# Second-layer weights of the first block group made among the last plain experts, in a pool of their own; two plain pairs exchanged; conversions of x begun at earlier steps

## The chip, the cores and the metric

One core of one Trainium2 chip runs the whole program. The metric is device microseconds from start to end of an execution; less is better. The engines are TensorE (PE, matrix products; PEld is its weight load), VectorE (DVE), ScalarE (ACT), GpSimd (POOL) and the queue of SyncE (SP), which issues the DMAs. Each engine works through its own instructions in a fixed order and waits, where it must, for semaphores of the others.

## The reference

```python
def _attn_ref(q, k, v, f_logit):             # (4, 8, 768, 48) each
    f = 1.0 / (1.0 + np.exp(-f_logit))
    for t in range(S):
        state = f[:, :, t, :, None] * state + np.einsum('bhd,bhe->bhde', k[:, :, t], v[:, :, t])
        y[:, :, t] = np.einsum('bhd,bhde->bhe', q[:, :, t], state)

def _moe_ref(x, w_gate, w1, w2):             # x is y as (3072, 384); 8 experts, 384 -> 1024 -> 384
    logits = x @ w_gate
    P = np.exp(logits - logits.max())
    for _ in range(8):
        P /= P.sum(1, keepdims=True) + 1e-09
        P /= P.sum(0, keepdims=True) + 1e-09
        P *= N / E
    for e in range(E):
        h = np.maximum(x @ w1[e], 0.0)
        ye = h @ w2[e]
        out += P[:, e:e + 1] * ye
```

A gated linear attention makes x. The gate's logits are balanced by eight rounds over rows and columns (P), and every expert is applied to every token, weighted with P.

## The kernel before

Everything is computed with pairs of fp16 numbers, a high part and a low part (names that end in h and l), and three products for one. The work has three stages, which overlap.

**Attention and tiles.** 24 steps of the recurrence make x as high and low parts (`xh`, `xl`, one pair of tiles for each of four batches b). While they run, products of the experts 0 and 1 with finished tokens fill TensorE.

**Plain experts.** Tokens come in eight units u, two for each batch. A *pair* (e, u) of `RAW` is expert e on unit u: eight first-layer groups (`hps`, 9 matmuls each, whose result ACT turns into `hh`, L423, and DVE into `hl`, L424) and three second-layer groups (`yps`, 24 matmuls each, which read all eight `hh` and `hl`). The order of matmuls is pinned: `mm` puts each behind the one before, and `pin` does the same on the other engines, so the order in which the Python code issues instructions is the order on each engine. Beside the last six pairs the main loop runs other generators, one piece of each per *step*. A step is 8 matmuls of the pairs (`LEAD`):

- `balance`, the eight rounds on P (L148 to L161; `sk_` names). In each round DVE makes column sums `sk_cs` (L153), TensorE adds them over partitions in one small product `sk_c`, which is issued in the pinned order 5 matmuls into the next step, and DVE goes on with its result (L157). At the end DVE makes `pes`.
- `convert(b)`, which turns x of a batch into the blocks that the third stage multiplies: `x32` = `xh` + `xl` (L1034, three instructions, on POOL for b = 0, 1 and on DVE for b = 2, 3), 17 sums on POOL (L1048, `xs`) with three maxima on DVE among them (L1051, `xmx`), and then high parts on ACT (L1067) and low parts on DVE (L1070: `xal` three times, `xbl` twice). `convert(0)` begins at step 0, the others at the steps in `CONVSTEP`. The low parts of a batch wait until its pairs are through, since they overwrite `xh` and `xl`.
- `prepare_w1` for the first two quarters of expert 2's first layer, at step `KSTEP`: a load (`k1r`), 10 sums on POOL (`k1s`), a maximum on DVE (L1105, `wmx`), ACT's high parts (L1112, `k1h`) and four low parts on DVE (L1115, `k1l`).

When the pairs up to the third from the end are issued, the pool with expert 0's weights is closed and the pool `kw` for `k1` opens in its space.

**Block groups.** For experts 2 to 7 the products are made by a scheme with 15 instead of 18 block products, in 48 *periods* n of 15 slots. In each slot TensorE multiplies into one of the banks `kb_A` to `kb_F`, and copies (ACT L1392), additions (DVE L1394, L1397, L1403) and splits (`kr`, `kf`, `kl`, `kgh`, `kgl`) follow after the slots as `EVENTS` says. From slot 18 on, matmuls of the second layer (`kyps`, `kxps`), which need `k2h` and `k2l`, are put between the slots. `prepare_w2` makes these: a load (`k2r`), a maximum on DVE (L1123), ACT's high parts (L1129, L1145), four sums on POOL (`k2s`) and three low parts on DVE (L1140, `k2l`). For the first two quarters of expert 2 its pieces stand in period 0, at the slots `W2AT0` and `W2AT1`; the other quarters follow in later periods.

Of the kernel before, what the change touches and what calls it, by code (L numbers as in the profile page):

```python
# [9 lines left out]
F16 = mybir.dt.float16  # L10
# [7 lines left out]
B, H, S, D = 4, 8, 768, 48  # L18
# [8 lines left out]
U = 2 * B  # L27
# [22 lines left out]
FLAG_AT = 0.5  # L50
RAW = [(e, u) for u in range(5) for e in range(2)] + [(0, 5), (0, 6), (0, 7), (1, 5), (1, 6), (1, 7)]
BALANCE = 2.0 ** 6
# [26 lines left out]
W1AT0 = (16, 18, 19, 19, 22, 23, 23, 27, 27, 32, 34, 40, 41)  # L79
W2AT0 = (0, 1, 2, 2, 3, 4, 6, 6, 8)  # L80
W2AT1 = (0, 1, 10, 10, 12, 13, 14, 14, 19)
W2AT3 = (0, 3, 6, 14, 16, 19, 20, 21, 26)
# [28 lines left out]
SECONDAT = ((12, 19), (12, 20), (15, 22), (21, 22), (21, 22), (22, 23), (25, 27), (25, 28))  # L111
CONVSTEP = (26, 53, 63)
KSTEP = 35
PUTOFF = 17
# [163 lines left out]
def fast(ctx, tc, qkf, vc, wg, w1, w2, out, flag):  # L278
# [667 lines left out]

    filler, credit = raw_pairs(RAW[:-3]), [0.0]

# [76 lines left out]
    xq = ctx.enter_context(tc.tile_pool(name="xq", bufs=1, reuse_waits="tile"))  # L1025
    accp = ctx.enter_context(tc.tile_pool(name="accp", bufs=B, reuse_waits="tile"))
    xc = {}

    def convert(b, raw_left):
# [29 lines left out]
        yield from wait(4)  # L1059
        while raw_left() > 0:  # L1060
            yield
# [58 lines left out]
    def prepare_w2(e, j):  # L1120
# [3 lines left out]
        yield  # L1124
        wh, wl = (lp.tile([128, 7, DH], F16, name=f"k2{n}_{e}_{j}", tag=f"k2{n}", bufs=4) for n in "hl")
        (b11, b12), (b21, b22) = ((raw[:, f, 0:DH], raw[:, f, DH:DM]) for f in range(2))
# [32 lines left out]

    last_pair = {u: max(n for n, p in enumerate(RAW) if p[1] == u) for u in range(U)}  # L1160
    done = [len(RAW) - 3]

    def raws():
        for e, u in RAW[-3:]:
            if (e, u) == RAW[-1]:
                banks[0] += (banks[0] + FT + TT) % 2 == 0
            yield from moe(e, u, ws[e])
            done[0] += 1

    def left(b):  # L1170
        return lambda: max(last_pair[2 * b], last_pair[2 * b + 1]) + 1 - done[0]

    def chained(gens):
        for gen in gens:
            yield from gen

    chain = balance()
    converts = [convert(b, left(b)) for b in range(B - 1)] + [convert(B - 1, lambda: RAW[-1] not in through)]
    work = [converts[0]]
    kw = None  # L1180
    step, held_mm = 0, None
    while True:
        more = fill(LEAD * 5 / 8)
        if held_mm:
            held_mm()
        more = fill(LEAD * 3 / 8)
        if not more and kw is None:
            wctx0.close()
            kw = ctx.enter_context(tc.tile_pool(name="kw", bufs=4, reuse_waits="tile"))
            filler = raws()  # L1190
            more = fill(0)
        if not more:
            break
        held_mm = next(chain, None)
        for gen in list(work):
            if next(gen, work) is work:
                work.remove(gen)
        step += 1
        if step in CONVSTEP:
            work.append(converts[1 + CONVSTEP.index(step)])  # L1200
        if step == KSTEP:
            work.append(chained(prepare_w1(ORDER[0][0], j, (5,)) for j in range(2)))
    while True:
# [3 lines left out]
        if held_mm == 0:  # L1207
            break
    for gen in work:
        for _ in gen:  # L1210
            pass
# [140 lines left out]
    for n, (e, m, b) in enumerate(ORDER):  # L1352
        part = n % 4
        if n + 4 < PERIODS and part in (0, 2):
            e2, m2, _ = ORDER[n + 4]
            gen = prepare_w1(e2, 2 * m2 + part // 2)
            at_all(n, W1AT if n else W1AT0, gen)
        if n == 0:
            at_all(0, W2AT0, prepare_w2(e, 2 * m))
            at_all(0, W2AT1, prepare_w2(e, 2 * m + 1))  # L1360
        if n - part + 4 < PERIODS and (n in (1, 3) if n < 4 else part in (0, 2)):
# [218 lines left out]
```

## Time and profile before

| | |
|---|---|
| median of 3 runs | 1453.34 us (1452.03 to 1453.49) |
| profiled execution, span from first to last instruction | 1451.7 us |
| what lies around the span, to the median | 1.6 us |
| mean granted TensorE clock | 0.998 |
| plain pairs beside which `balance` and `convert` run | about 353 to 472 us |
| period 0 of the block groups begins | 471.8 us |

The median of the runs is the number to compare with. The profiled execution's own time, as far as the profile tells it, is its span; the 1.6 us between it and the median are start, end and the spread of the runs. Times in the rows further down are microseconds from the span's start. Two instructions of one engine may overlap a little in the profile, so the price of an instruction in a full queue is read from its start to the next one's start.

### The profile page before, as it was taken

To read this page: it belongs to the slowest core of one execution; us is meant where nothing else is said; L and a number is where in the kernel's file an instruction comes from. 1 tells how busy PE (TensorE), PEld (TensorE's weight loads), DVE (VectorE), ACT (ScalarE), POOL (GpSimd) and SP (SyncE) were. 2 spreads that over 40 slices of the span, in tenths; PEclk is the share of its full clock that TensorE was granted. 3 is DMA by queue.
4 is the path that set the end of the run, shared out by engine and by line. 5 is a ranking of instruction groups with operands and counts; after the bars stand their busy time and mean duration, and the time that the engine had idled before them with its cause. 6 is when DMAs were issued, how large, how long until landed. Compare 5 with 4: busy or idle time off the path is not lost.

```text
span 1451.7 us, 40369 instructions
## 1 busy us (share of the span) xinstructions
PE 1439.9 (99%) x16050; PEld 1256.9 (87%) x16050; DVE 1229.0 (85%) x2511; ACT 1060.4 (73%) x2381; POOL 1047.8 (72%) x1230
## 2 busy tenths in 40 slices
PE   8999999999999999999999999999999999999998
PEld 5888876666666899999999999999999999999998
DVE  8888787885787899888899989888898888888876
ACT  7766667663344877888888888888877877788765
POOL 4334434446439576999999999999998888888766
PEclk9999999999999999999999999999999999999999
DMA  9455455551010101222211121111111100000012
GB/s 282 112 136 128 120 137 121 123 116 38 28 34 33 40 24 24 57 62 62 59 59 50 51 61 40 45 51 56 50 34 34 34 23 25 20 14 24 2 45 90
DMA packets 105684, 92.36 MB, mean 64 GB/s; under 512 B 72256, under 2 KB 92448, under 8 KB 105488
## 3 DMA queue, kind: packets, MB, share of 16 engines
q1 hardware_dynamic: 104912, 89.33, 22.5%
q8 instruction: 126, 2.06, 0.6%
q14 instruction: 70, 0.57, 0.1%
q10 hardware_dynamic: 576, 0.39, 0.1%
HBM read 63.84 MB, written 14.16 MB: 54 GB/s over the span
## 4 chain that ended last, share of the span: by engine, by line
PE 96%; DVE 2%; ACT 1%; issue 0%; DMA 0%; DVEq 0%; SPq 0%; ACTq 0%
PE kyps L306 29%; PE yps L306 15%; PE hps L306 12%; PE kb_A L306 9%; PE kb_B L306 8%; PE kb_D L306 6%; PE kxps L306 5%; PE kb_C L306 4%; PE kb_E L306 2%; PE kb_F L306 2%; PE aps L306 1%; PE kvps L306 1%; DVE hl L478 0%; PE low L306 0%; PE lps L306 0%
## 5 line engine op out<-in xcount | busy, mean ns | idle before, releaser
L306 PEld LDWEIGHTS <-k1h 128*128 128x128 f16 x2880 | 270.9, 98 | 21.3 <-issue 2.7
L306 PE MATMUL kyps<-k2l,kgh 128*128 128x192 f16 x1146 | 281.9, 246 | 0.0
L306 PE MATMUL kyps<-k2h,kgh 128*128 128x192 f16 x1146 | 281.9, 246 | 0.0
L306 PE MATMUL kyps<-k2h,kgl 128*128 128x192 f16 x1146 | 281.9, 246 | 0.0
L306 PEld LDWEIGHTS <-kgh 128*128 128x128 f16 x2304 | 212.0, 98 | 6.3
L1441 POOL TENSOR_TENSOR kgl<-kf,kgh 128x512 f16<-128x512 f32 x144 | 192.1, 1334 | 2.0 <-ACT kgh L1438 2.0
L1441 POOL TENSOR_TENSOR kgl<-kr,kgh 128x512 f16<-128x512 f32 x144 | 178.6, 1240 | 11.0 <-ACT kgh L1438 10.9
L1260 DVE SCALAR_TENSOR_TENSOR yy<-kyps,pes,part 128x192 f32<-128x192 f32 x258 | 107.1, 415 | 89.9 <-PE kyps L306 79.9
L1314 POOL TENSOR_TENSOR acc<-acc,yy 128x384 f32<-128x384 f32 x129 | 128.9, 1000 | 56.1 <-DVE yy L1260 56.1
L306 PEld LDWEIGHTS <-k1l 128*128 128x128 f16 x1440 | 140.9, 98 | 16.3
L306 PE MATMUL yps<-w2h,hl 128*128 128x384 f16 x384 | 125.1, 326 | 0.5 <-DVE hl L478 0.5
L306 PE MATMUL yps<-w2h,hh 128*128 128x384 f16 x384 | 125.3, 326 | 0.1
L306 PE MATMUL yps<-w2l,hh 128*128 128x384 f16 x384 | 125.2, 326 | 0.0
L306 PEld LDWEIGHTS <-w1h 128*128 128x128 f16 x1344 | 96.9, 98 | 32.0 <-ACT w1h L374 0.4
L306 PEld LDWEIGHTS <-kh 128*128 128x128 f16 x1152 | 108.1, 98 | 6.4
L306 PEld LDWEIGHTS <-kgl 128*128 128x128 f16 x1152 | 112.7, 98 | 0.2 <-issue 0.2
L306 PEld LDWEIGHTS <-hh 128*128 128x128 f16 x768 | 73.7, 98 | 44.6 <-issue 0.9
L1257 ACT ACTIVATE kyps<-kyps 128x192 f32<-128x192 f32 x143 | 45.3, 317 | 80.4 <-PE kyps L306 78.9
L1438 ACT ACTIVATE kgh<-kf 128x512 f16<-128x512 f32 x144 | 91.9, 638 | 0.5 <-DVE kf L1415 0.3
L1438 ACT ACTIVATE kgh<-kr 128x512 f16<-128x512 f32 x144 | 91.7, 637 | 0.0
L1392 ACT ACTIVATE cp<-kb_A 128x512 f32<-128x512 f32 x144 | 86.3, 599 | 2.7 <-DVE kb_A L1394 2.0
L1418 POOL TENSOR_TENSOR kr<-kr 128x256 f32<-128x256 f32 x96 | 71.7, 747 | 17.2 <-ACT kr L1407 14.2
(310 smaller groups left out, 5251.4 us busy)
## 6 DMA issues: line engine op xcount, KB each, us to landing
q<-in_qkf_dram SPq DMA_DIRECT2D x23, 672.0 KB, 5.5
k1r<-in_w_dram SPq DMA_DIRECT2D x24, 384.0 KB, 3.0
ys<-yr SPq DMA_DIRECT2D x48, 192.0 KB, 2.1
k2r<-in_w_dram SPq DMA_DIRECT2D x24, 384.0 KB, 3.1
yb<-ys SPq DMA_DIRECT2D x48, 192.0 KB, 2.3
vr<-in_vc_dram SPq DMA_DIRECT2D x24, 192.0 KB, 4.7
out_dram<-acc SPq DMA_DIRECT2D x20, 192.0 KB, 1.9
w1r<-in_w_dram SPq DMA_DIRECT2D x8, 384.0 KB, 7.9
```

The lines of the kernel that those rows point to most:

```text
L306: ins = (nc.tensor.transpose if transpose else nc.tensor.matmul)(**kw)
L1257: pin(nc.scalar.activation(out=out, in_=in_, func=AF.Copy, **kw))
L1260: pin(nc.vector.scalar_tensor_tensor(out=y, in0=ps, scalar=p, in1=z, op0=ALU.mult, op1=ALU.add))
L1314: pin(nc.gpsimd.tensor_tensor(out=y, in0=y, in1=z.rearrange("p s d -> p (s d)"), op=ALU.add))
L1392: pin(nc.scalar.activation(out=fresh(ev[2]), in_=bk, func=AF.Copy))
L1418: pin((nc.gpsimd if ev[2] == 'P' else nc.vector).tensor_tensor(out=r[:, 0], in0=r[:, 1], in1=r[:, 0], op=ALU.subtract))
L1438: pin(nc.scalar.activation(out=hs['g', t][0][i], in_=hs['f' if i else 'r', t], func=AF.Copy))
L1441: pin(nc.gpsimd.tensor_tensor(out=hs['g', t][1][i], in0=hs['f' if i else 'r', t], in1=hs['g', t][0][i], op=ALU.subtract))
```

## The change

`RAW` is reordered: the pair (1, 5) now comes before (0, 6), (0, 7), (1, 6), (1, 7) and no longer after (0, 7). Two pairs instead of three are held back (`HELD`) for the time after expert 0's weights are closed. `kw` is opened earlier, beside those weights. The space of expert 0's weights goes to a new pool `kp`, in which all `k2` tiles live; before, they lived in `lp`. `CONVSTEP` moves the conversions of batches 1, 2, 3 from steps 26, 53, 63 to 18, 37, 53. The first layer's preparation begins at step 27 (`K1STEP`) and no longer at 35. The two second-layer preparations of expert 2 leave period 0 and begin 6 and 17 steps after `kp` opens (`K2AFTER`).

```diff
-RAW = [(e, u) for u in range(5) for e in range(2)] + [(0, 5), (0, 6), (0, 7), (1, 5), (1, 6), (1, 7)]
+RAW = [(e, u) for u in range(6) for e in range(2)] + [(0, 6), (0, 7), (1, 6), (1, 7)]
+HELD = 2
...
-W2AT0 = (0, 1, 2, 2, 3, 4, 6, 6, 8)
-W2AT1 = (0, 1, 10, 10, 12, 13, 14, 14, 19)
...
-CONVSTEP = (26, 53, 63)
-KSTEP = 35
+CONVSTEP = (18, 37, 53)
+K1STEP = 27
+K2AFTER = (6, 17)
...
-    filler, credit = raw_pairs(RAW[:-3]), [0.0]
+    filler, credit = raw_pairs(RAW[:-HELD]), [0.0]
...
+    kw = ctx.enter_context(tc.tile_pool(name="kw", bufs=4, reuse_waits="tile"))
+    kp = []
...
-        wh, wl = (lp.tile([128, 7, DH], F16, name=f"k2{n}_{e}_{j}", tag=f"k2{n}", bufs=4) for n in "hl")
+        wh, wl = (kp[0].tile([128, 7, DH], F16, name=f"k2{n}_{e}_{j}", tag=f"k2{n}") for n in "hl")
...
     def left(b):
-        return lambda: max(last_pair[2 * b], last_pair[2 * b + 1]) + 1 - done[0]
+        return lambda: any(u // 2 == b and u >= TILED and (e, u) not in through for e, u in RAW)
...
+    begun = {}
+    for at_, gen in zip(CONVSTEP, converts[1:]):
+        begun.setdefault(at_, []).append(gen)
+    begun.setdefault(K1STEP, []).append(chained(prepare_w1(ORDER[0][0], j, (5,)) for j in range(2)))
...
-        if not more and kw is None:
+        if not more and not kp:
             wctx0.close()
-            kw = ctx.enter_context(tc.tile_pool(name="kw", bufs=4, reuse_waits="tile"))
+            kp.append(ctx.enter_context(tc.tile_pool(name="kp", bufs=4, reuse_waits="tile")))
+            for j, after in enumerate(K2AFTER):
+                begun.setdefault(step + after, []).append(prepare_w2(ORDER[0][0], j))
             filler = raws()
...
-        if step in CONVSTEP:
-            work.append(converts[1 + CONVSTEP.index(step)])
-        if step == KSTEP:
-            work.append(chained(prepare_w1(ORDER[0][0], j, (5,)) for j in range(2)))
+        work += begun.pop(step, [])
...
-        if n == 0:
-            at_all(0, W2AT0, prepare_w2(e, 2 * m))
-            at_all(0, W2AT1, prepare_w2(e, 2 * m + 1))
```

TensorE's own order keeps its shape: the same groups of matmuls in the same places, with `sk_c` after the same matmul each time; only which expert and unit a group is for has changed. Three places show what the other engines get. The names in them are those above; a number behind a name counts buffers.

The first place is DVE between the fifth and the sixth `sk_c` of the eight, beside the fourth-last pair. Before:

```order
L1070 TENSOR_TENSOR xbl_7357<-xs_0_7359,xbh_7356 128x512
L161 TENSOR_TENSOR pe<-pe,sk_cs 128x192
L148 TENSOR_REDUCE sk_rs<-pe 128x24
L149 TENSOR_SCALAR sk_rs<-sk_rs 128x24
L150 RECIPROCAL sk_rs<-sk_rs 128x24
L1070 TENSOR_TENSOR xbl_7357<-xs_0_7359,xbh_7356 128x512
L152 TENSOR_TENSOR pe<-pe,sk_rs 128x192
L153 TENSOR_REDUCE sk_cs<-pe 128x8
```

and in the changed program:

```order
L1072 TENSOR_TENSOR xbl_7360<-xs_0_7362,xbh_7359 128x512
L1053 TENSOR_REDUCE xmx<-x_1_7581 128x1
L161 TENSOR_TENSOR pe<-pe,sk_cs 128x192
L148 TENSOR_REDUCE sk_rs<-pe 128x24
L149 TENSOR_SCALAR sk_rs<-sk_rs 128x24
L150 RECIPROCAL sk_rs<-sk_rs 128x24
L1072 TENSOR_TENSOR xbl_7360<-xs_0_7362,xbh_7359 128x512
L1053 TENSOR_REDUCE xmx<-x_1_7581 128x1
L152 TENSOR_TENSOR pe<-pe,sk_rs 128x192
L153 TENSOR_REDUCE sk_cs<-pe 128x8
```

Two maxima of batch 1 (`xmx`) have come between, ahead of the column sums; a third one stands just ahead of these rows.

The second place is DVE between the seventh and the eighth `sk_c`, beside the second-layer matmuls of the third-last pair. Before, from DVE's first use of the seventh `sk_c` to the column sums for the eighth:

```order
L157 TENSOR_SCALAR sk_cs<-sk_c_7898 128x8
L158 RECIPROCAL sk_cs<-sk_cs 128x8
L159 TENSOR_SCALAR sk_cs<-sk_cs 128x8
L161 TENSOR_TENSOR pe<-pe,sk_cs 128x192
L148 TENSOR_REDUCE sk_rs<-pe 128x24
L149 TENSOR_SCALAR sk_rs<-sk_rs 128x24
L150 RECIPROCAL sk_rs<-sk_rs 128x24
L152 TENSOR_TENSOR pe<-pe,sk_rs 128x192
L153 TENSOR_REDUCE sk_cs<-pe 128x8
```

and in the changed program, from the second row of that use to the same column sums:

```order
L158 RECIPROCAL sk_cs<-sk_cs 128x8
L159 TENSOR_SCALAR sk_cs<-sk_cs 128x8
L1072 TENSOR_TENSOR xbl_7635<-xs_1_7637,xbh_7634 128x512
L1036 TENSOR_TENSOR x_2_7905<-xh_4428,xl_4429 128x768
L161 TENSOR_TENSOR pe<-pe,sk_cs 128x192
L148 TENSOR_REDUCE sk_rs<-pe 128x24
L149 TENSOR_SCALAR sk_rs<-sk_rs 128x24
L150 RECIPROCAL sk_rs<-sk_rs 128x24
L1107 TENSOR_REDUCE wmx<-k1r_1_7923 128x1
L1053 TENSOR_REDUCE xmx<-x_2_7905 128x1
L152 TENSOR_TENSOR pe<-pe,sk_rs 128x192
L153 TENSOR_REDUCE sk_cs<-pe 128x8
```

A low part of batch 1, one addition for batch 2, the maximum of `k1r` and a maximum of batch 2 now stand among them. From `hl` of the third-last pair's first group to these column sums there are 8 instructions of 768 elements, 2 `xbl` and 4 `k1l` in the changed program that don't belong to the pair or to `balance`, and 3 instructions of 768 elements before.

The third place is DVE in period 0, from slot 13 to the end of bank B. Before:

```order
L1397 TENSOR_TENSOR kb_F<-kb_D,cp_1_8617 128x512
L1415 SCALAR_TENSOR_TENSOR kr_0_8656<-kb_B,kr_0_8656 128x256
L1415 SCALAR_TENSOR_TENSOR kf_0_8695<-kb_B,kr_0_8656 128x256
L1140 SCALAR_TENSOR_TENSOR k2l_1_8676<-k2r_1_8565,k2h_1_8675 128x192
L1403 TENSOR_TENSOR cp_3_8722<-kb_D,cp_4_8574 128x512
L1415 SCALAR_TENSOR_TENSOR kf_0_8695<-kb_B,kf_0_8695 128x256
L1446 SCALAR_TENSOR_TENSOR kl_0_8551<-kb_B,kh_0_8550 128x512
```

and in the changed program:

```order
L1394 TENSOR_TENSOR kb_F<-kb_D,cp_1_8637 128x512
L1412 SCALAR_TENSOR_TENSOR kr_0_8673<-kb_B,kr_0_8673 128x256
L1412 SCALAR_TENSOR_TENSOR kf_0_8704<-kb_B,kr_0_8673 128x256
L1400 TENSOR_TENSOR cp_3_8728<-kb_D,cp_4_8605 128x512
L1412 SCALAR_TENSOR_TENSOR kf_0_8704<-kb_B,kf_0_8704 128x256
L1443 SCALAR_TENSOR_TENSOR kl_0_8586<-kb_B,kh_0_8585 128x512
```

The `k2l` is gone, and so are its five fellows further up and down and two maxima; nothing else has moved there. On ACT six high parts and on POOL the eight sums `k2s` have left period 0 in the same way. In the changed program the `k2l` stand on DVE after the third `xmx` of batch 3 and between the `hl` of the last pair. On SP the loads of `k1r_0`, `k1r_1` and `k2r_0` stand far ahead, as before; that of `k2r_1` stands one store of `yr` later than before, and that of `k1r_2` four stores earlier.

## Rows read from the trace of the kernel before

**Rows 1.** The page, part 1: busy us (share of span) xinstructions of TensorE.
```profile
PE 1439.9 (99%) x16050; PEld 1256.9 (87%) x16050; DVE 1229.0 (85%) x2511; ACT 1060.4 (73%) x2381; POOL 1047.8 (72%) x1230
```

**Rows 2.** Windows: stretch, length, busy us (xinstructions) per engine, PEclk, DMA share, GB/s.
```profile
400.00:425.00 25.00, 25.00 (x159) 15.37 (x157) 22.11 (x50) 11.81 (x24) 8.30 (x14) 1.00 0.07 24
...
475.00:500.00 25.00, 23.09 (x215) 19.68 (x213) 20.57 (x41) 21.41 (x46) 17.28 (x25) 1.00 0.16 49
500.00:525.00 25.00, 24.50 (x262) 23.09 (x261) 22.64 (x50) 19.38 (x45) 17.06 (x26) 1.00 0.01 2
```

**Rows 3.** Timeline of PE: start us, us, engine line op out<-in; balance products.
```profile
399.44 0.28 PE L306 MATMUL sk_c<-sk_cs,onesf 128*128 128x8 f32 x2
...
419.35 0.28 PE L306 MATMUL sk_c<-sk_cs,onesf 128*128 128x8 f32 x2
```

**Rows 4.** Timeline of DVE: the column sums that two balance products read.
```profile
397.92 0.50 DVE L153 TENSOR_REDUCE sk_cs<-pe 128x8 f32<-128x192 f32 x1
...
416.73 0.50 DVE L153 TENSOR_REDUCE sk_cs<-pe 128x8 f32<-128x192 f32 x1
```

**Rows 5.** Timeline of DVE: instructions back to back, for their prices.
```profile
405.59 0.95 DVE L1051 TENSOR_REDUCE xmx<-x 128x1 f32<-128x768 f32 x1
...
434.12 0.82 DVE L1115 SCALAR_TENSOR_TENSOR k1l<-k1s,k1h 128x640 f16<-128x640 f32 x1
434.86 0.95 DVE L1034 TENSOR_TENSOR x<-xh,xl 128x768 f32<-128x768 f16 x1
435.72 0.55 DVE L424 SCALAR_TENSOR_TENSOR hl<-hps,hh 128x384 f16<-128x384 f32 x1
436.19 0.42 DVE L1115 SCALAR_TENSOR_TENSOR k1l<-k1r,k1h 128x256 f16<-128x256 f32 x1
436.52 0.95 DVE L1034 TENSOR_TENSOR x<-xh,xl 128x768 f32<-128x768 f16 x1
```

**Rows 6.** Timeline of DVE: instructions beside running POOL instructions.
```profile
394.66 0.88 DVE L161 TENSOR_TENSOR pe<-pe,sk_cs 128x192 f32<-128x192 f32 x1
...
421.68 0.67 DVE L1115 SCALAR_TENSOR_TENSOR k1l<-k1r,k1h 128x256 f16<-128x256 f32 x1
422.27 0.61 DVE L161 TENSOR_TENSOR pe<-pe,sk_cs 128x192 f32<-128x192 f32 x1
```

**Rows 7.** Timeline of POOL in the same microseconds.
```profile
422.03 0.63 POOL L1103 TENSOR_TENSOR k1s<-k1r,k1s 128x128 f32<-128x128 f32 x1
```

**Rows 8.** Windows early in the program, for the granted clock (PEclk).
```profile
24.00:26.00 2.00, 1.35 (x30) 1.11 (x31) 1.97 (x4) 2.00 (x6) 1.57 (x3) 1.00 1.04 402
26.00:28.00 2.00, 2.00 (x14) 1.22 (x15) 1.79 (x3) 1.74 (x4) 1.88 (x3) 0.69 1.05 403
28.00:30.00 2.00, 2.00 (x6) 0.87 (x6) 1.77 (x4) 0.60 (x2) 0.16 (x1) 0.50 1.06 301
```

**Rows 9.** Timeline of PE in the first periods of the block groups.
```profile
482.29 0.27 PE L306 MATMUL kb_D<-xah,k1l 128*128 128x256 f16 x1
...
484.34 0.28 PE L306 MATMUL kb_B<-xbh,k1h 128*128 128x256 f16 x1 [0.47 <-DVE kl L1446]
...
491.00 0.24 PE L306 MATMUL kyps<-k2l,kgh 128*128 128x192 f16 x1
...
508.27 0.27 PE L306 MATMUL kb_A<-xbh,k1h 128*128 128x256 f16 x1 [0.50 <-ACT cp L1392]
```

**Rows 10.** Timeline of DVE in the same periods.
```profile
482.27 0.49 DVE L1140 SCALAR_TENSOR_TENSOR k2l<-k2r,k2h 128x192 f16<-128x192 f32 x1
482.68 0.68 DVE L1403 TENSOR_TENSOR cp<-kb_D,cp 128x512 f32<-128x512 f32 x1
...
483.61 0.68 DVE L1446 SCALAR_TENSOR_TENSOR kl<-kb_B,kh 128x512 f16<-128x512 f32 x1
...
489.84 1.11 DVE L1140 SCALAR_TENSOR_TENSOR k2l<-k2s,k2h 128x768 f16<-128x768 f32 x1
...
506.16 0.82 DVE L1115 SCALAR_TENSOR_TENSOR k1l<-k1s,k1h 128x640 f16<-128x640 f32 x1
```

More of the change, by code (lines that the diff above doesn't have):

```diff
@@ L1059, in convert @@
         yield from wait(4)
-        while raw_left() > 0:
+        while raw_left():
             yield
@@ L1158, in first_maxima @@
                     yield
-    last_pair = {u: max(n for n, p in enumerate(RAW) if p[1] == u) for u in range(U)}
-    done = [len(RAW) - 3]
     def raws():
-        for e, u in RAW[-3:]:
+        for e, u in RAW[-HELD:]:
             if (e, u) == RAW[-1]:
@@ L1167, in raws @@
             yield from moe(e, u, ws[e])
-            done[0] += 1
     def left(b):
-        return lambda: max(last_pair[2 * b], last_pair[2 * b + 1]) + 1 - done[0]
+        return lambda: any(u // 2 == b and u >= TILED and (e, u) not in through for e, u in RAW)
     def chained(gens):
@@ L1177, in fast @@
     chain = balance()
-    converts = [convert(b, left(b)) for b in range(B - 1)] + [convert(B - 1, lambda: RAW[-1] not in through)]
+    converts = [convert(b, left(b)) for b in range(B)]
     work = [converts[0]]
-    kw = None
+    begun = {}
+    for at_, gen in zip(CONVSTEP, converts[1:]):
+        begun.setdefault(at_, []).append(gen)
+    begun.setdefault(K1STEP, []).append(chained(prepare_w1(ORDER[0][0], j, (5,)) for j in range(2)))
     step, held_mm = 0, None
@@ L1208, in fast @@
             break
-    for gen in work:
+    for gen in work + [gen for at_ in sorted(begun) for gen in begun[at_]]:
         for _ in gen:
```

## The prediction

> **What bounds the kernel now.** I read the page's totals first, then the windows, and then the timelines of the engines that TensorE waits for. The totals say where time can come from at all: TensorE is busy for 1439.9 of 1451.7 us [rows 1], so its own order of matmuls is the program, and nothing on another engine counts unless TensorE waits for it. The windows say where it waits [rows 2]. Beside the plain pairs it doesn't wait (25.00 of 25 us from 400 on), although DVE is busy for 22.11 us there. In period 0 and the start of period 1 it does: 1.91 us idle in 475 to 500, 0.50 us in 500 to 525. The change takes work out of the second place and puts it into the first. So two questions decide: how much of the 2.4 us is the `k2` work's doing, and whether the first place has room.
>
> **What period 0 gives back.** The idle time is not the whole loss. A matmul's modelled end lies behind the next one's start (a bank's matmuls begin 0.11 us apart and show 0.27 us), so each wait hides a further 0.16 us; for the ten waits that is 1.6 us, 4.0 us in all. That is the most the change can win.
>
> A large one of these waits shows how little hangs on `k2`. `kb_B` at 484.34 waits for `kl` on DVE [rows 9], which began at 483.61, behind a queue in which `k2l` stood at 482.27 for 0.41 us [rows 10]. Without it the next instruction, the sum that reads `kb_D`, could start earlier; but that sum must wait for slot 13's last matmul into `kb_D`, which began at 482.29 and shows 0.27 us, so to 482.56 [rows 9]. It started at 482.68; without `k2l` it starts at about 482.61. The win is 0.07 us, and `kl`, `kb_B` and the copies behind them move by as much. This is how period 0 is built: with no second-layer matmuls between its slots, each slot waits for a chain of copy, addition and next slot. At 491.00 a second-layer matmul waits for `k2l`, which ran from 489.84 for 1.11 us; its gap to the one before is 0.26 us instead of 0.08, so 0.18 us go away. The wait at 508.27 stands behind DVE's `k1l` at 506.16 [rows 10], which stays. I take 0.25 us as the gain; its ends are 0.1 and 4.0 us.
>
> **What the place beside the pairs costs.** DVE's queue counts here, because TensorE's pinned order holds the `sk_c` products: each waits for the column sums that DVE makes in its turn. The eighth one starts at 419.35 [rows 3], and its sums were done at 416.73 + 0.50 = 417.23 [rows 4]: 2.1 us to spare. The sixth one starts at 399.44, its sums were done at 398.42: 1.0 us to spare. This is the room.
>
> Prices in a full queue, from start to start [rows 5]: 0.86 us for an instruction of 768 elements (434.86 to 435.72; the maxima have the same 0.95 us of duration), 0.74 for `k1l` of 640, 0.33 for 256, and between these 0.47 for 384; for `xbl` of 512 elements two thirds of 0.86, 0.58.
>
> Sixth `sk_c`: the three maxima of batch 1 now stand ahead of its sums, 3 x 0.86 = 2.6 us. The sums are done at 398.42 + 2.6 = 401.0, which is 1.6 us late.
>
> Seventh and eighth: from the first `hl` of the third-last pair to the eighth's sums, the order now has 8 instructions of 768 elements (6.9 us), two `xbl` (1.2) and four `k1l` (0.74 + 0.74 + 0.33 + 0.47 = 2.3), 10.4 us, where 3 of 768 elements stood (2.6): 7.8 us more. The sums would be done at 417.23 + 7.8 = 425.0 against 419.35, 5.7 us late. The whole lateness at the eighth is TensorE's loss, whichever of the products it falls on. To this comes the 1.6 us, since the first `hl` of that pair waits for TensorE; against it, some 0.4 us of small idle pieces of DVE in that stretch are filled. That makes 6.8 us.
>
> The lower end is 5.2 us (the 1.6 us don't carry over). The upper end has collisions. At 421.68 a `k1l` of 256 elements took 0.59 us to the next start instead of 0.33, with POOL's `k1s` beside it [rows 6, 7], and L161 took 0.88 us at 394.66 and 0.61 at 422.27. In the changed program the ten sums of the second `k1s` fall beside the stretch itself; at a quarter of a microsecond for each of two to seven colliding instructions this is 0.5 to 1.8 us, so the upper end is 8.6 us. I take 7.3. The Trainium skill, "SBUF — State Buffer", section "SBUF: two separate sides", says that a DVE instruction with two inputs in SBUF and a GpSimd instruction that reads SBUF take one port by turns, the second being blocked until the first is done; the lengthened rows agree.
>
> What else is moved is covered. The maxima and low parts of `k2` on DVE (two of 768, then 192, 384 and 768 elements twice) stand after the last `sk_c`, beside the last two pairs. The tightest place is the last pair but one, where three additions, three `xal` and a maximum stand between four `hl`: 7 x 0.86 and 4 x 0.47, 7.9 us, against some 8.4 us until the second layer wants its last `hl`; a collision there would cost tenths. ACT's high parts and POOL's sums of `k2` have nobody waiting until period 0's second layer. On SP, `k2r_1` waits for a buffer that the `k1l` give up before the next store is due, and behind `k1r_2`, which waits for `k2l`, stands one store of `yr` that isn't made yet. The exchange of pairs gives TensorE the same matmuls.
>
> **The clock.** Of the loss at the seventh and eighth `sk_c`, 5.7 us together, the larger part, about 4 us, is one unbroken wait, as most of the added work stands between these two. Nothing in the trace stops TensorE so long. The nearest is at 24 to 26, where it was busy for 1.35 of 2.00 us; after that the granted clock was 0.69 in 26 to 28 and 0.50 in 28 to 30 [rows 8], that is 1.2 GHz instead of 2.4, and 0.31 x 2 + 0.50 x 2 = 1.6 us of work were lost. The short waits of 475 to 500 left it at 1.00 [rows 2]. I take it that the long wait costs these 1.6 us too. The Trainium skill, "TensorE: Matmul & The Clock Gate", section "Why this matters for your kernels", says that idle gaps between matmul bursts bring the clock back to half; rows 8 agree, and rows 2 show that short ones don't. It speaks against this change.
>
> **The sum.** Against the profiled execution: 1451.7 + 7.3 + 1.6 - 0.25 = 1460.35. The median lies 1.64 above that execution's span, so 1462.0 us.
>
> **The rivals.**
> 1. *Late sums with the clock kept.* 1453.34 + 7.3 - 0.25 = 1460.4. For it: the wait may be cut by matmuls between the seventh and eighth product more evenly than I think. Against: rows 8.
> 2. *Late sums at the lower end, clock kept.* 1453.34 + 5.2 - 0.25 = 1458.3, if DVE's prices hold without collisions and the sixth product's lateness is absorbed.
> 3. *Faster.* Period 0's waits are the `k2` work's after all, on ACT rather than on DVE, and all of them go: 1453.34 - 4.0 = 1449.3. For it: ACT is busy for 21.41 of 25 us in 475 to 500 [rows 2]. Against: the chains above. It needs DVE beside the pairs to be less than 1.1 us late (4.0 less the 2.9 us that are 0.2%), while I count at least 5.2.
> 4. *No change.* Both are half true: the sums are 5.2 us late and period 0 gives back 3 to 4 us, 1453.34 + 5.2 - 3.5 = 1455.0.
>
> **How the numbers follow.** Forecast (late sums and the clock) 0.50, rival 1 0.23, rival 2 0.12, rival 4 0.08, rival 3 0.05; and 0.02 for still later sums with two falls of the clock, 1453.34 + 8.6 + 3.2 = 1465.1. A change of 0.2%, 2.9 us, is about what a measurement of this kernel tells from none. So slower has 0.87, the same 0.08, faster 0.05. The range goes from 1457.3 (rival 2 less a microsecond of gain in period 0) to 1465.1, and leaves out rivals 3 and 4.
>
> **What would show it.** In the changed profile, TensorE should have three waits for `sk_cs` of DVE, beside the fourth-last and third-last pairs: about 1.6 us, then 1.5 to 2, then about 4, the last at some 423 us and with a granted clock of 0.5 soon after it. Period 0 should begin at about 480.5 instead of 471.8, and its waits for `kb_A`, `kb_B` and `kb_D` should be there as before, with only the second-layer matmul's wait gone. DVE should have no idle time worth the name from the first `hl` of the third-last pair on. The forecast is wrong if TensorE passes the eighth `sk_c` before 422 us, or if the waits of period 0 have shrunk by more than a microsecond.

## The result and the profile after

The changed kernel takes 1461.07 us in the median of 5 runs (1459.83 to 1462.26), against 1452.03 us (1451.69 to 1453.49) for the kernel before on the same chip: a ratio of 1.0062, 95% interval 1.0049 to 1.0074. It is 0.6% slower, and the forecast of 1462.0 us lies 0.9 us above the median. As a difference, 8.65 us was forecast (the median of before was 1453.34 us then) and 9.04 us was measured. The profiled execution has a span of 1460.5 us; the prediction's sum for it was 1460.35.

One word has to be put right first. The product that starts at 399.44 us before [rows 3] is the fifth of the eight `sk_c`. The section on the change puts the place ahead of it between the fifth and the sixth, the prediction and several expectations call it the sixth, and one expectation calls the fourth the fifth. The places, rows and numbers are those meant; only the count was off, and the seventh and eighth are counted rightly. The text below counts from one to eight.

The page's totals, answering to [rows 1]:

```profile
PE 1444.7 (99%) x16050; PEld 1257.9 (86%) x16050; DVE 1228.8 (84%) x2511; ACT 1060.2 (73%) x2381; POOL 1044.0 (71%) x1230
```

The same number of matmuls, 4.8 us more of busy time: TensorE did some of them slowly. The rest of the loss is waiting.

The waits of TensorE, longest sum first (engine, its output, line, what was waited for: us in all, times, longest):

```profile
PE sk_c L306 <- DVE sk_cs L153: 4.8, 3, 2.4
...
PE kb_A L306 <- ACT cp L1389: 1.1, 3, 0.5
```

The first line is new: three waits for the column sums. The second belongs to period 0 and period 1 and is the same as before. Here are the products on TensorE's timeline, with the idle time in front of them in brackets, answering to [rows 3]:

```profile
393.18 0.28 PE L306 MATMUL sk_c<-sk_cs,onesf 128*128 128x8 f32 x2
...
400.69 0.39 PE L306 MATMUL sk_c<-sk_cs,onesf 128*128 128x8 f32 x2 [0.71 <-DVE sk_cs L153]
...
415.96 0.39 PE L306 MATMUL sk_c<-sk_cs,onesf 128*128 128x8 f32 x2 [1.73 <-DVE sk_cs L153]
...
426.90 0.59 PE L306 MATMUL sk_c<-sk_cs,onesf 128*128 128x8 f32 x2 [2.35 <-DVE sk_cs L153]
```

The fourth product (393.18) stands 0.38 us later than in the profile of before, where it starts at 392.80; that difference comes from the program's start and is taken off. Then the fifth is 400.69 - 399.44 - 0.38 = 0.87 us late, and the eighth 426.90 - 419.35 - 0.38 = 7.17 us. The sums they wait for, on DVE, answering to [rows 4]:

```profile
400.13 0.50 DVE L153 TENSOR_REDUCE sk_cs<-pe 128x8 f32<-128x192 f32 x1
...
426.35 0.50 DVE L153 TENSOR_REDUCE sk_cs<-pe 128x8 f32<-128x192 f32 x1
```

The second is done at 426.85, and the product starts 0.05 us behind it. The windows of that stretch (busy us and number of instructions of PE, PEld, DVE, ACT, POOL, then PEclk) show what the waits do to the clock:

```profile
414.00:416.00 2.00, 0.27 (x3) 0.04 (x1) 1.97 (x6) 0.14 (x1) 1.84 (x4) 1.00 0.00 0
416.00:418.00 2.00, 2.00 (x9) 1.04 (x10) 2.00 (x3) 0.49 (x1) 1.92 (x4) 0.58 0.03 8
418.00:420.00 2.00, 2.00 (x9) 0.98 (x7) 2.00 (x4) 0.00 (x0) 1.08 (x1) 0.56 0.00 0
...
424.00:426.00 2.00, 0.55 (x4) 0.10 (x1) 1.97 (x5) 1.99 (x6) 2.00 (x4) 1.00 0.10 35
426.00:428.00 2.00, 1.10 (x5) 0.76 (x6) 1.93 (x6) 0.00 (x0) 2.00 (x4) 0.64 0.00 0
428.00:430.00 2.00, 2.00 (x8) 0.99 (x7) 1.93 (x4) 0.00 (x0) 2.00 (x4) 0.50 0.00 0
```

DVE is busy for 1.93 to 2.00 of every 2 us, TensorE is nearly idle in 414 to 416, and the granted clock falls toward half twice: behind the seventh product (0.58 and 0.56, each the mean of 2 us) and behind the eighth (0.64 and 0.50). Period 0 and the start of period 1, answering to the last two of [rows 2]:

```profile
475.00:500.00 25.00, 23.17 (x185) 17.49 (x184) 12.95 (x27) 13.92 (x28) 8.30 (x14) 1.00 0.09 29
500.00:525.00 25.00, 24.50 (x261) 23.05 (x259) 19.95 (x42) 19.80 (x47) 14.71 (x23) 1.00 0.01 1
```

The `k2` work is gone from there, but TensorE's idle time is 1.83 + 0.50 = 2.33 us where it was 1.91 + 0.50 = 2.41. Period 0 begins later in the changed kernel, so the windows don't hold the same work, but both hold the same eight waits (0.09 to 0.5 us). The gain is read better from the first matmul of period 0 to the last of these waits, which is at 508.27 before [rows 9]. That first matmul before, on TensorE's timeline:

```profile
471.81 0.27 PE L306 MATMUL kb_A<-xbh,k1h 128*128 128x256 f16 x1
```

and both in the changed kernel:

```profile
480.95 0.27 PE L306 MATMUL kb_A<-xbh,k1h 128*128 128x256 f16 x1
...
517.16 0.27 PE L306 MATMUL kb_A<-xbh,k1h 128*128 128x256 f16 x1 [0.51 <-ACT cp L1389]
```

This stretch takes 517.16 - 480.95 = 36.21 us where it took 508.27 - 471.81 = 36.46: period 0 gives back 0.25 us.

So the time went as follows. Up to the eighth product 0.38 + 7.17 us were lost. From it to period 0 TensorE needs 480.95 - 426.90 = 54.05 us where it needed 471.81 - 419.35 = 52.46; that 1.59 us is what the second slow stretch cost. With the 0.25 us given back the sum is 8.89 us. The spans differ by 8.8, so 0.1 us is left to the rest of the program.

### The profile page after: what moved, and what is told of

Same layout as the page of the kernel before. It is cut to its first block, busy times and chain, and to the rows that moved or that the text cites. A ratio compares the mean times of both kernels' runs of the same rounds, so it can differ in the third digit from the quotient of the medians.

```text
span 1460.5 us, 40368 instructions
## 1 busy us (share of the span) xinstructions
PE 1444.7 (99%) x16050; PEld 1257.9 (86%) x16050; DVE 1228.8 (84%) x2511; ACT 1060.2 (73%) x2381; POOL 1044.0 (71%) x1230
## 4 chain that ended last, share of the span: by engine, by line
PE 92%; DVE 5%; ACT 1%; DMA 1%; issue 1%; SPq 0%; DVEq 0%; ACTq 0%
PE kyps L306 29%; PE yps L306 14%; PE hps L306 11%; PE kb_A L306 8%; PE kb_B L306 8%; PE kb_D L306 6%; PE kxps L306 5%; PE kb_C L306 4%; PE kb_E L306 2%; PE kb_F L306 2%; PE aps L306 1%; PE kvps L306 1%; DMA w2r<-in_w_dram 1%; DVE k1l L1117 0%; DVE xal L1072 0%
```

## The experiments

Twelve kernels ran, five times or more each beside runs of the kernel before. The median is given, with its ratio to the kernel before and the 95% interval of that; what a timeline shows is from one execution. Edits are to the changed kernel if nothing else is said. The lateness of a product is counted from the first `sk_c` of the same execution (372.89 us before), so that the start of the program drops out. Two stretches of before are used again: 52.46 us from the eighth product to period 0, and 36.46 us from there to the last of the eight waits.

**1. Conversions and k1 at their old steps.** The `k2` work, its pool and the new order stay.

```
-CONVSTEP = (18, 37, 53)
-K1STEP = 27
+CONVSTEP = (26, 53, 63)
+K1STEP = 35
```

> Keeps the move of the k2 work, its pool and the new order of pairs; puts the conversions of x and the k1 work back to the steps they had before. Ahead of every one of the eight column sums DVE then has the same work as in the kernel before. Theory (the conversions and k1 begun sooner are the whole loss, period 0 hardly gains): no wait for sk_cs, TensorE passes the eighth sk_c at about 419.4 us, the clock stays at 1.00 beside the pairs, period 0 gains only 0.25 us: about 1451.8 us, the same as before. Rival A (the k2 work beside the last pairs, the pool or the new order is what costs): over 1454 us. Rival B (period 0's waits are k2's after all and the gain was drowned by the late sums): about 1448 us.

Measured: 1459.17 us against 1452.19, ratio 1.0051 (1.0037 to 1.0064). The waits for `sk_cs` are gone, as expected, but the time hardly is: undoing these steps doesn't bring back the 1451.8 us of the theory. Whether they are the whole loss of the changed kernel is settled by experiments 2 and 7. TensorE now waits in the last pair, and from the eighth product, which is in time, to period 0 it needs 59.65 us for 52.46. Its timeline there:

```profile
464.03 0.34 PE L306 MATMUL yps<-w2h,hh 128*128 128x384 f16 x1 [2.64 <-ACT hh L423]
...
467.24 0.50 PE L306 MATMUL yps<-w2h,hl 128*128 128x384 f16 x1 [1.48 <-DVE hl L424]
```

ACT's timeline, the instruction that holds up that `hh`:

```profile
462.75 0.84 ACT L1147 ACTIVATE k2h<-k2s 128x768 f16<-128x768 f32 x1 [7.14 <-POOL k2s L1138]
463.50 0.47 ACT L423 ACTIVATE hh<-hps 128x384 f16<-128x384 f32 x1
```

And POOL's, which makes what this instruction reads:

```profile
453.01 3.65 POOL L1050 TENSOR_TENSOR xs<-x 128x256 f32<-128x256 f32 x3
...
458.30 1.85 POOL L1135 TENSOR_TENSOR k2s<-k2r 128x192 f32<-128x192 f32 x2
...
461.47 1.25 POOL L1138 TENSOR_TENSOR k2s<-k2r,k2s 128x192 f32<-128x192 f32 x2
```

ACT's order has `k2h_1` in front of the pair's last three `hh`. It needs POOL's `k2s`, which stand among the sums of x, and POOL does nothing but these from 448 on. So ACT sits idle for 7.14 us with an `hh` behind the waiting instruction. Ahead of the `hl` of the second wait DVE has `k2l_1`, 1.47 us at 465.24. Behind the first wait the clock falls, to 0.57 in 464 to 466 and 0.50 from 466 to 470.

**2. k2 back in period 0.** `begun` gets no `prepare_w2`, and period 0 calls it with the old `W2AT0` and `W2AT1`; conversions, k1 and the order of pairs stay as changed.

> Keeps the conversions of x and k1 begun sooner and the new order of pairs; puts the k2 work back into period 0 at its old places. Theory: the three waits for sk_cs stay at 0.9, 1.9 and 2.5 us, TensorE passes the eighth sk_c at about 426.9 us, period 0 loses its 0.25 us again: about 1461.3 us. Rival A (k2 beside the last pairs costs): 1453 to 1459 us. Rival B (period 0 had gained much by the move): 1463 us or more.

Measured: 1461.03 us, ratio to before 1.0060 (1.0047 to 1.0074), the changed kernel's 1461.07 within the spread. Here the three waits for `sk_cs` sum to 5.5 us. The eighth product is 7.17 us late, as in the changed kernel. Beside early conversions it makes no difference to the time where the `k2` work is done, as far as an interval of some 2 us to either side can tell; in the profile, the stretch in period 0 takes 36.47 us here and 36.21 in the changed kernel.

**3. TensorE kept busy in the waits.**

```
+            products += 1
+            warm({7: 8, 8: 18}.get(products, 0))
```

`products` counts the `sk_c`, and `warm(n)` issues n matmuls of 512 columns into a bank that nobody reads.

> The changed kernel with matmuls into an unread bank put just ahead of the seventh sk_c (8 of 512 columns) and of the eighth (18), so that TensorE is not idle while it waits there. The sums themselves are as late as before. Theory (the first fall of the clock cost nothing, the second about 1.5 us): the granted clock stays at 1.00 from 414 to 432, the eighth sk_c starts at about 426.9 as in the changed kernel, and the whole is about 1.5 us shorter, 1459.6 us. If both falls cost as much as the clock alone says (1.7 us each): about 1457.7 us. If neither costs: 1461.1 us.

Measured: 1459.63 us, ratio 1.0052 (1.0038 to 1.0066), 1.44 us less than the changed kernel (the intervals of the two overlap), with the granted clock at 1.00 in every window from 412 to 432. The eighth product starts at 425.61, which with this profile's start (first product 371.29 for 372.89) is 7.9 us late. Its column sums are done at 424.39 + 0.50 + 1.60 = 426.49 on the scale of before; in the changed kernel it was 426.85 - 0.38 = 426.47. A clock kept through the seventh wait doesn't bring them forward, and the inserted matmuls themselves end 0.7 us too late. The way from the eighth product to period 0, on TensorE's timeline:

```profile
425.61 0.29 PE L306 MATMUL sk_c<-sk_cs,onesf 128*128 128x8 f32 x2
...
478.07 0.27 PE L306 MATMUL kb_A<-xbh,k1h 128*128 128x256 f16 x1
```

It takes 52.46 us, as much as before and 1.59 less than in the changed kernel. So of the two falls one counts, 1.6 us. During the first, TensorE ran slowly only toward a product whose sums weren't there yet.

**4. Batch 2 converted late.**

```
-CONVSTEP = (18, 37, 53)
+CONVSTEP = (18, 53, 63)
```

> The changed kernel with only the conversion of batch 2 begun at step 53 and of batch 3 at 63, as before. Three additions and a maximum of 768 elements each leave DVE's queue ahead of the eighth column sums: 4 x 0.86 = 3.4 us. Theory: the waits at the sixth and seventh sk_c stay as in the changed kernel (0.9 and 1.9 us), the eighth sk_c starts at about 426.9 - 3.4 = 423.5 us, and the time is about 1457.6 us, or 1456.1 if the clock doesn't fall a second time. Rival (what delays the eighth sums is not the number of DVE's instructions ahead of them but a wait for TensorE, ACT or POOL): 1460 us or more.

Measured: 1463.16 us, ratio 1.0077 (1.0064 to 1.0091), slower still. What the theory said of the eighth product held: it starts at 421.40, and with its first product 1.58 us earlier than before's (371.31 for 372.89) it is 421.40 - 419.35 + 1.58 = 3.6 us late, where 7.17 - 3.4 = 3.8 was counted. Its time did not hold: the last pair waits as in experiment 1 (`yps` for `hh` 1.0 us and for `hl` 1.8 us, then the slow clock), which costs more than the 3.5 us that were saved.

**5 and 6. The second k2 chunk behind the last hh.** Experiment 1, and experiment 4, each with

```
-K2AFTER = (6, 17)
+K2AFTER = (6, 30)
```

> The first experiment (conversions and k1 at their old steps) lost time at a place that I had costed at nothing: ACT's k2h_1 stands ahead of the last three hh of the last pair and waits 7.1 us for POOL's k2s_1, which is behind POOL's sums of x. This kernel is that one with the second k2 chunk begun 30 steps after the pool is there instead of 17, so that ACT's k2h_1 stands behind the last hh; nothing else is changed. Theory: the wait at 461 and 465 us (2.9 + 1.9 us), the slow clock behind it (about 2 us) and so all 7.2 us go; period 0 keeps its gain of about 0.25 us: about 1451.9 us, the same as before. Rival A (DVE's part of k2, not ACT's queue, delays the last pair): 1455 us or more, with waits for hl. Rival B (k2l_1, now later, holds back period 0's second layer): 1453.5 us or more, with a wait for k2l in period 0.

> The fourth experiment (conversion of batch 2 begun late) with the second k2 chunk begun 30 steps after the pool is there, so that the last pair's wait goes. What stays are the column sums' delays as the fourth showed them, 0.9 + 1.9 + 0.7 = 3.5 us, with the clock at 1.00 throughout. Theory: 1452.2 + 3.5 - 0.25 = 1455.4 us. Rival (part of the fourth's loss is of another kind): 1458 us or more.

Measured: 1456.66 us (ratio 1.0030, 1.0019 to 1.0041) and 1457.85 us (1.0039, 1.0026 to 1.0052). No wait is left in the last pair, so the place of the second chunk was the cause there. Its parts on DVE and POOL moved too; that ACT's queue made the first wait is read from the timelines of experiment 1. But of the 7 us of experiment 1 only 2.5 are back. The wait went one place on. ACT, in experiment 5, behind the pairs:

```profile
473.61 0.84 ACT L1147 ACTIVATE k2h<-k2s 128x768 f16<-128x768 f32 x1 [2.71 <-POOL k2s L1138]
474.36 0.58 ACT L1389 ACTIVATE cp<-kb_A 128x512 f32<-128x512 f32 x1
```

Now `k2h_1` stands ahead of period 0's first `cp`, TensorE waits 3.2 us for that, and the clock is 0.50 in 476 to 478; the stretch in period 0 takes 41.27 us for 36.46. In experiment 6 the wait is 1.4 us and the clock stays at 1.00. Its sum fits: 1451.95 (the kernel before beside it) + 3.5 for the column sums + 1.4 - 0.25 = 1456.6; two of its runs had a mean clock of 1.000 and took 1456.83 and 1457.05 us. The median is about a microsecond above these.

**7. The order of pairs and the pools alone.** Experiment 2 with the old `CONVSTEP` and `K1STEP`.

> Of the change only the exchange of two plain pairs, the pool of its own and the kw pool opened sooner; the conversions, k1 and k2 where they were before. Theory: these cost nothing: no wait beside the pairs, 1452.2 us. Rival (the order of the pairs or the pools hold back a load or a weight): 1454 us or more.

Measured: 1452.05 us, ratio 1.0003 (0.9994 to 1.0012). These parts cost nothing that the interval shows. Between this kernel and experiment 2 only the steps of the conversions and of k1 differ, and both have the `k2` work in period 0: that is 9.0 us, as much as the changed kernel loses.

**8. k1 late, conversions early.** `K1STEP = 35` and `K2AFTER = (6, 30)`.

> The changed kernel with only the k1 work put back to step 35, and the second k2 chunk begun 30 steps after the pool is there (so that ACT's queue is not what counts). Ahead of the eighth column sums four k1l (2.3 us) and a maximum (0.86 us) leave DVE's queue, 3.1 us; ahead of the seventh three k1l and the maximum (2.7 us). POOL's k1s go from beside this stretch too. Theory: the sixth sk_c is late as before (0.9 us), the seventh hardly, and the eighth starts about 3.1 us sooner than in the changed kernel, at some 423.8 us, 4.4 us later than before; 1456.4 us with the clock kept, up to 1457.9 if it falls in the one long wait of about 3 us. Rival (the conversions alone are the whole loss): 1460 us or more. Rival (k1 alone is the whole loss): 1453 us or less.

Measured: 1466.06 us, ratio 1.0088 (1.0075 to 1.0101), the slowest of all. The eighth product is 4.8 us late (expected 4.4). The rest I had not expected: the k1 work came out in the next pair, on ACT as `k1h` ahead of `hh`, and on DVE with everything else. ACT's timeline:

```profile
434.10 0.74 ACT L1114 ACTIVATE k1h<-k1s 128x640 f16<-128x640 f32 x1 [1.69 <-POOL k1s L1105]
434.74 0.47 ACT L423 ACTIVATE hh<-hps 128x384 f16<-128x384 f32 x1
437.65 0.74 ACT L1114 ACTIVATE k1h<-k1s 128x640 f16<-128x640 f32 x1 [2.43 <-POOL k1s L1105]
```

And TensorE's, which waits for `hl`:

```profile
448.91 0.34 PE L306 MATMUL yps<-w2h,hl 128*128 128x384 f16 x1 [2.73 <-DVE hl L424]
...
451.28 0.50 PE L306 MATMUL yps<-w2h,hl 128*128 128x384 f16 x1 [1.71 <-DVE hl L424]
```

From 452 to 456 the clock is 0.50.

**9 and 10. k1 begun much sooner.** If DVE and POOL are full from 400 on, room must be looked for ahead of it. `K1STEP = 8`, with `CONVSTEP = (26, 44, 54)` in the first, `(26, 53, 63)` in the second.

> The runs so far put the loss down to DVE and POOL being full from about 400 us to the end of the pairs: whatever is begun sooner makes the column sums late, whatever is begun later comes out at the last pairs or at period 0's first copies. In the kernel before, DVE is busy for only 4.70 of 10 us from 370 and POOL idle from 380 to 390. This kernel is the changed one with the k1 work begun at step 8 (at about 370 us) instead of 27, and the conversions of batches 1 to 3 at steps 26, 44 and 54, so that ahead of the sixth to eighth column sums DVE has only k1 work added, done long before. Theory: the sums are in time (no wait for sk_cs over 0.2 us), POOL has room for the k2 sums before the last pair, no wait for hh, hl or the first cp; the k2 work is then free, and period 0 gains its 0.25 us: about 1451.8 us, same as before. Rival A (the early k1 work makes the third to fifth column sums late, which had 0.6 to 1 us to spare): 1453 to 1454.5 us, with waits for sk_cs between 385 and 400 us. Rival B (POOL is still too late for k2s_1): 1454 us or more, with a wait for hh in the last pair.

> As the kernel beside it (k1 begun at step 8), but with the conversions at their old steps 26, 53 and 63. DVE and POOL have no k1 work left from 396 on, but the additions for x_2 and x_3 still begin as late as in the kernel before, and POOL's sums of x with them. Theory (what delays the last pair is POOL's sums of x_2 and x_3 and the k2 sums behind them, which can't start sooner than the additions): the wait for hh in the last pair stays, 1456 us or more. Rival (it was the k1 work that filled POOL and DVE there): no wait, about 1452 us.

Measured, beside 1453.35 us for the kernel before: 1459.41 us (ratio 1.0042, 1.0028 to 1.0055) and 1464.61 us (1.0078, 1.0065 to 1.0092). The second kept the waits of the last pair, as its theory said. The first lost them nearly, but the fourth product waits 4.1 us in both; rival A's place, at several times the 1 to 2 us that it was given. DVE's timeline in experiment 9 ahead of that product:

```profile
388.67 0.64 DVE L161 TENSOR_TENSOR pe<-pe,sk_cs 128x192 f32<-128x192 f32 x1
389.23 2.39 DVE L1072 TENSOR_TENSOR xal<-xs,xah 128x768 f16<-128x768 f32 x1
...
393.52 1.40 DVE L152 TENSOR_TENSOR pe<-pe,sk_rs 128x192 f32<-128x192 f32 x1
394.96 0.50 DVE L153 TENSOR_REDUCE sk_cs<-pe 128x8 f32<-128x192 f32 x1
```

POOL's timeline beside it:

```profile
383.26 0.98 POOL L1105 TENSOR_TENSOR k1s<-k1r 128x128 f32<-128x128 f32 x2 [19.13 <-DVE k1l L1117]
...
389.05 5.66 POOL L1036 TENSOR_TENSOR x<-xh,xl 128x768 f32<-128x768 f16 x3
```

POOL had waited 19.13 us for the single buffer of `k1s` (the `k1l` of the first chunk read it), and its three additions for batch 1, behind that in its order, ran beside DVE's part of the balance. `xal` took 2.39 us, the multiplication of 192 elements 1.40.

**11 and 12. The two k1 chunks apart.** Experiment 9 with the first chunk at step 8 and the second at step 40, behind the eighth column sums; the last also with `K2AFTER = (6, 30)`.

```
-    begun.setdefault(K1STEP, []).append(chained(prepare_w1(ORDER[0][0], j, (5,)) for j in range(2)))
+    for at_, j in zip(K1STEPS, range(2)):
+        begun.setdefault(at_, []).append(prepare_w1(ORDER[0][0], j, (5,)))
```

> In the kernel with k1 begun at step 8, POOL's sums for the second k1 chunk waited for their buffer until 383 us, so POOL's three additions for batch 1 ran at 389 to 394.7 instead of 361 to 366; beside them DVE's xal took 2.39 us instead of 0.95 and the multiplication ahead of the fifth sums 1.40 instead of 0.35, and TensorE waited 4.1 us. Here only the first k1 chunk begins at step 8, the second at step 40, behind the eighth column sums; the rest is as in that kernel. Theory (POOL's additions beside DVE's were the cause): POOL adds batch 1 at about 366 to 371, no wait for sk_cs, and what stays is the wait for hl in the last pair of 0.7 us (0.9 us lost): about 1452.7 us, that is 6 us less than that kernel. Rival A (k1 work on DVE at that place is itself the cause): 1455 us or more, with a wait for sk_cs before 400 us. Rival B (the second chunk fills DVE and POOL at the last pairs as in the tenth experiment): 1456 us or more, with waits for hl.

> As the kernel beside it, with the second k2 chunk begun 30 steps after its pool is there instead of 17, behind ACT's last hh. Theory: with the conversions ended by 470 us POOL makes those sums before period 0's first copies, so the wait for hl goes and none takes its place: 1452.0 us, the same as the kernel before within 0.1%. Rival (the second chunk holds up ACT's first copy as in the seventh experiment): 1454 us or more, with a wait of TensorE for cp at the start of period 0.

Measured: 1457.32 us (ratio 1.0036, 1.0024 to 1.0049) and 1452.89 us (ratio 1.0009, 1.0000 to 1.0018). In both POOL adds batch 1 at about 364 to 369, and no wait for `sk_cs` over 0.2 us is left. DVE's timeline in experiment 12, the two instructions that were long:

```profile
388.46 0.95 DVE L1072 TENSOR_TENSOR xal<-xs,xah 128x768 f16<-128x768 f32 x1
...
390.73 0.36 DVE L152 TENSOR_TENSOR pe<-pe,sk_rs 128x192 f32<-128x192 f32 x1
```

The `k1l` of the first chunk are still beside them, so the collision with POOL was the cause. Experiment 11 was still 4.6 us above its forecast. Its profiled execution, at 1455.85 us, loses 3.6 us between the eighth product and period 0, where the forecast had 0.9: `k2h_1` again held up the last `hh` (ACT waited 5.98 us for `k2s`), and the pair before waited 1.2 us for an `hl`. Why the median is 1.5 us longer than this execution is not shown. Experiment 12 takes the first away, and TensorE's windows are nearly full up to period 0:

```profile
400.00:425.00 25.00, 25.00 (x160) 15.42 (x158) 20.47 (x48) 12.30 (x25) 3.04 (x7) 1.00 0.07 24
425.00:450.00 25.00, 25.00 (x156) 15.04 (x155) 22.48 (x30) 11.62 (x26) 24.58 (x26) 1.00 0.10 32
450.00:475.00 25.00, 24.38 (x157) 15.14 (x155) 15.31 (x21) 11.60 (x24) 12.73 (x17) 1.00 0.25 82
```

It is the changed kernel but for the steps at which work begins, and 8.2 us faster. It doesn't beat the kernel before: with nearly all `k2` work taken out of period 0 and almost no wait put in its place, the time is 0.1% above that of before, by 1.04 us. Beside the pairs and in period 0 two waits of TensorE are new, on its timeline:

```profile
453.69 0.65 PE L306 MATMUL hps<-xh,w1h 128*128 128x384 f16 x3 [0.30 <-DVE hl L424]
...
473.25 0.27 PE L306 MATMUL kb_A<-xah,k1h 128*128 128x256 f16 x1 [0.32 <-ACT cp L1390]
```

The second is for the first `cp` of period 0, ahead of which `k2h_1` stands on ACT here too. In this execution the eighth product is 0.26 us late, the way to period 0 takes 52.92 us for 52.46, and the stretch in period 0 36.69 for 36.46. Together this is 0.95 us, nearly all of the remainder.

## Why the prediction was right, and where its reasons were not

**Column sums late: right, and nearly to size.** Taken at the eighth product the loss was put at 7.3 us and is 7.17. Its parts were off in opposite directions. The carry-over from the fifth was put at 1.6 us and is 0.87. The three maxima are there and DVE works without a break in both kernels, but four instructions ahead of the sums that had run long before (L159, L161, `xbl` and L152, 2.97 us together) take 2.09 us here, so the sums came 1.8 us later and not 2.6. The seventh and eighth were put at 5.7 us, less 0.4, plus 0.5 for collisions, 5.8 in all, and lost 7.17 - 0.87 = 6.3. The last step, of "about 4 us", is 7.17 - 2.87 = 4.3 us (the seventh is 415.96 - 412.71 - 0.38 = 2.87 us late), but not the one unbroken wait that was predicted: a wait of 2.35 us, and the rest TensorE's slow passage in front of it. That the total comes so near is luck in part. Experiment 4 checks the price: four instructions of 768 elements fewer, 7.17 - 3.6 = 3.5 us less lateness, where 3.4 us were counted.

**The clock: right in sum, wrong in picture.** One fall and 1.6 us were predicted. There were two in the profiled execution, and the first cost nothing. The second cost 1.59 us; experiment 3 takes it away and needs the 52.46 us of before. That the size agrees so well is luck in part, as it was carried over from a stretch at the program's start: behind the longer last wait of experiment 2 (3.06 us) the same way takes 54.25 us, 1.79 more than before. The Trainium skill, "TensorE: Matmul & The Clock Gate", section "Why this matters for your kernels", warns of idle gaps between matmul bursts; the windows above agree, but the cases don't follow from a wait's length alone. The same wait of 1.73 us at the seventh product was followed by a clock of 0.58 here and by 1.00 in experiments 2 and 4, and two of the changed kernel's five runs (1460.49 and 1459.83 us) had a mean clock of 1.000.

**Period 0 gives back next to nothing: right, and to size.** 0.25 us was taken, and 36.46 - 36.21 = 0.25 us was measured. The other kernels agree: with the `k2` work in period 0 the stretch takes 36.47 and 36.46 us (experiments 2 and 7), without it 36.20 to 36.22 (1, 3, 4, 9, 10 and 11). Rival 3 (faster, period 0's waits are `k2`'s) is refuted: in the changed kernel the `k2` work is gone from there, and all eight waits are left. Those over 0.1 us are for `cp`, `kb_F`, `kf` and `kl`, which are links of the chain of slot, copy and addition. The prediction counted ten waits for its bound of 4.0 us; with eight the bound is 2.4 + 8 x 0.16 = 3.7 us, which moves rivals 3 and 4 a little and not the forecast.

**"What else is moved is covered": wrong as a reason, true by luck of the steps.** The prediction said that ACT's high parts and POOL's sums of `k2` have nobody waiting before period 0. Nobody waits for their results, but ACT's `hh` stand behind them in its order. In the changed kernel the early conversions let POOL make `k2s_1` in time: ACT waited 0.75 us for it at 466.30, and TensorE didn't notice. In experiments 1, 4, 10 and 11 the same instruction made TensorE wait. So what the changed kernel loses is the doing of the conversions and k1 begun sooner, as experiments 2 and 7 show, and its `k2` work costs nothing that can be seen. But with these at their old steps the `k2` work loses 7 us by itself (experiment 1), at another place, so the two prices don't add. That one reason lies behind both is argued from the timelines: DVE ahead of the column sums (busy for 1.93 to 2.00 of every 2 us) and POOL beside the last pairs (busy for 29.84 of the 30 us from 440 to 470 in the kernel before) had no room for one more chunk, and each single move back only chose who waits, `sk_c` (the changed kernel), `hh` (1), `cp` (5) or `hl` (8).

**The rivals.** The time alone doesn't tell the forecast from rival 1, the clock kept (1460.4): that lies 0.7 us below the median, and the interval reaches 1.8 us to either side. The granted clock tells them apart, for the profiled execution, and the two runs with a mean clock of 1.000 are rival 1's case. The lower end (1458.3) and no change (1455.0) lie below the interval.

## What to carry to other kernels

Before moving work, ask of every engine not only who needs the moved result, but what stands behind the moved instruction on its engine, and what it waits for itself: a high part that nobody needed yet kept ACT idle for 7 us with an `hh` behind it. When undoing a part doesn't bring the loss back, look where the wait went; a crowded stretch has to be relieved ahead of it, here by beginning some work 40 us sooner (`k1s` at 356.5 us in experiment 12, at 396.8 before). And a slow clock cost only what the next late result didn't hide: nothing behind the seventh product, 1.6 us behind the eighth.

## What the runs showed that I had not expected

DVE and POOL instructions hinder each other far more than the quarter of a microsecond that the prediction took from [rows 6, 7]. Beside POOL's additions of 768 elements (5.66 us for three), DVE's `xal` took 2.39 us instead of 0.95 and a multiplication of 192 elements 1.40 instead of 0.36, and POOL's three took 4.84 us where they ran elsewhere (experiments 11 and 12). What was added to DVE's instructions, 1.44 and 1.04 us, is less than one POOL addition (1.9 us) each time. The Trainium skill, "SBUF — State Buffer", section "SBUF: two separate sides", says that such a pair shares one port as a lock that the first holds for its whole instruction; experiment 9 agrees. By these two rows, and they are few, the price goes by POOL's instruction and not by DVE's.
